# Attention and two gated layers on one core: nine groups of instructions put behind later ones in the order of emission

## The chip, the cores and the metric

The kernel runs on one core of a Trainium2 chip. The metric is the device time of one execution in microseconds (us). A core has five engines that work at the same time, each through its own instructions in order: PE (matrix products), DVE (VectorE), ACT (ScalarE), POOL (GpSimd) and SP (here only the queue that issues transfers). They wait for each other, and for transfers, through semaphores.

## What is computed

```python
# attention: a window of 15 keys to each side, and the 24 block summaries of all keys
k_sum, v_sum = k blocks of 32: max, mean
a = softmax(concat([masked q k^T, q k_sum^T + log 32]))      # 2 batches, 8 heads, 768 rows, 64 wide
x = (a @ concat([v, v_sum]))                                 # 1536 tokens x 512
# first layer
xn = x / sqrt(mean(x * x) + 1e-6) * rms_g
x = (silu(xn @ w_gate) * (xn @ w_val)) @ w_out               # 512 -> 1536 -> 512
# second layer
h = x @ w_in2
out = where(h > 0, h, exp(min(h, 0)) - 1) @ w_out2           # 512 -> 2048 -> 512
```

The weights come as float64. Queries and keys are scaled so that the softmax is sharp.

## The kernel before

The 1536 tokens are three blocks of 512. Block 0 goes through both layers alone, chunk by chunk of 128 columns (`add_block1`, `add_block2`); blocks 1 and 2 go through them together afterwards, by seven products in place of eight (`add_joint`). Attention works on pairs of 64 query rows: the pair `j` of a batch is one score product (`scores`), and for each half `h` of the heads the row maxima (`row_max`, tile `nm`), the exponentials (`exps`, tile `e`, sums in `ss`), `guard` and `invert` (the factor `rs`), `normalize` (`e` times `rs`, on POOL or on DVE), four transposes (`turn_e`, tile `at`), a copy to SBUF (`copy_e`, tile `ats`), then the product with the values (`apply_v2`, tile `pv`) and a copy into the block (`copy_x2`, tile `xT`). The names carry batch, pair and half: `e_2_0` is the third pair's first half. Pairs 0 to 3 of batch 0 are block 0; pair 4 is the first of block 1.

A product in float32 is made of three: each operand is split in a high part (`x_hi` for the block, `split_a` for a weight) and what is left (`x_lo`, `split_b`), tiles `xs` and `ws`. Block 0 is split in halves of 256 tokens, since its first two chunks (`pg` for the gate, `pv_0c`, `pv_1c` for the value) start when the first half is there.

A weight of 128 x 512 float64 words is made float32 in four steps after its transfer (`st`): `convert_a` on ACT, `convert_b` on DVE (sign, exponent and all but three bits of the mantissa, into tile `raw`), `convert_c` for some, and `convert_d` on DVE, which adds the three lowest bits of the mantissa. `raw` is then split, and `keep` on SP writes it to HBM, from where blocks 1 and 2 load it again (`kept`).

The norm's root is found per half of block 0: two `square` on ACT, `sum_square` on PE (eight products with four columns each, tile `pss`), `mean_square` on DVE (`ms`), `root` on POOL (`y`), `diagonal` on DVE (`dg`), `spread` on PE (`prs`), `keep_root` (`rk`). For block 0 the root is not applied to `x`; it enters behind the first products, in `gate_r`, which needs both halves of `rk`.

The order of work is made by a planner (class `Order`): each group of instructions has an engine, a cost, a due time (shifted by the table `SHIFT`) and the tiles that it reads and writes. The planner plays the engines through time and appends each group to `started` when it begins; PSUM banks and buffers are given out in the same play. At the end of `Order.issue` the groups are emitted in the order of `started`:

```python
        for i in started:
            ops[i][3](*((taken[i],) if isinstance(ops[i][0], dict) else ()), *ops[i][4])
```

The engine's own order is the order of emission. The semaphores are set at emission too: an instruction waits for the last writer of what it reads, and for readers and writers of what it overwrites, as far as those have been emitted before it. A tile that takes over a PSUM bank or a buffer waits for the last user emitted before it.

Of the kernel before, what the change touches and what calls it, by code (L numbers as in the profile page):

```python
# [43 lines left out]
class Order:  # L44
# [18 lines left out]
    def add(self, engine, cost, due, fn, *args, r=(), w=(), new=()):  # L63

        due += SHIFT.get((fn.__name__, sum(due >= x for x in EDGES)), 0)
        self.ops.append((engine, cost, due, fn, args, tuple(r), tuple(w), tuple(new)))
# [15 lines left out]
    def issue(self):  # L82
        ops = self.ops
        n = len(ops)
        before = [set() for _ in range(n)]
        writer, readers, home, maker, users = {}, {}, {}, {}, {}
        queue = {}
        for i, (engine, _, due, _, _, r, w, new) in enumerate(ops):
            for tag, name in new:
                home[name] = tag  # L90
                if tag in self.slots and self.slots[tag][1]:
                    queue.setdefault(tag, []).append((due, i, name))
            for key in r:
                before[i].add(writer[key])
                readers.setdefault(key, []).append(i)
            for key in w:
                if key in writer:
                    before[i].add(writer[key])
                before[i].update(readers.pop(key, ()))
                writer[key] = i  # L100
            before[i].discard(i)
            for name in {key.split("#")[0] for key in (*r, *w)} | {name for _, name in new}:
                if name in home:
                    before[i].add(maker.setdefault(name, i))
                    users.setdefault(name, set()).add(i)
            before[i].discard(i)
        queue = {tag: [name for _, _, name in sorted(x)] for tag, x in queue.items()}
        after = [[] for _ in range(n)]
        left = [len(b) for b in before]
        for i, b in enumerate(before):  # L110
            for j in b:
                after[j].append(i)

        ready_at = [op[2] if op[0] in ("SP", "-") else 0.0 for op in ops]
        free = {tag: bufs for tag, (bufs, _) in self.slots.items()}
        busy, soon, started, port = dict(self.busy), {}, [], 0.0
        dma_free = now = 0.0
        events = [(t, -1, 0) for t in (*ready_at, *busy.values()) if t > 0]
        heapq.heapify(events)
        taken = [None] * n  # L120
        ticks = {}
        tiled = 0

        def offer(i):
            for engine in ops[i][0] if isinstance(ops[i][0], dict) else (ops[i][0],):
                soon.setdefault(engine, []).append(i)

        for i in range(n):
            if not left[i]:
                offer(i)  # L130


        def pick(i):
            need, found = {}, []
            for tags, name in ops[i][7]:
                for tag in tags if isinstance(tags, tuple) else (tags,):
                    n = need.get(tag, 0) + 1
                    if free[tag] >= n and (not self.slots[tag][1] or name in queue[tag][:n]):
                        break
                else:  # L140
                    return None
                need[tag] = n
                found.append((tag, name))
            return found

        def can(i):
            return pick(i) is not None

        def shared(i, engine):
            return engine in ("DVE", "POOL") and ops[i][3].__name__ in SHARED  # L150

        while len(started) < n or events:
            for engine in list(soon):
                if busy.get(engine, 0.0) > now + 1e-9:
                    continue
                todo = sorted((i for i in soon[engine] if taken[i] is None), key=lambda i: (ops[i][2], i))
                best = next((
                    i for i in todo if ready_at[i] <= now + 1e-9 and can(i)
                    and (not shared(i, engine) or port <= now + 1e-9)), None)
                if best is None:  # L160
                    continue
                where, cost, due, _, _, _, _, new = ops[best]
                if isinstance(where, dict):
                    cost = where[engine]
                look = now + self.look * cost
                if engine != "SP" and any(
                        ops[i][2] < due - self.urgent and now < ready_at[i] <= look and can(i) for i in todo):
                    continue
                taken[best] = engine
                for e in where if isinstance(where, dict) else (where,):  # L170
                    soon[e].remove(best)
                for tag, name in pick(best):
                    home[name] = self.tag_of[name] = tag
                    free[tag] -= 1
                    if self.slots[tag][1]:
                        queue[tag].remove(name)
                if engine == "SP":
                    dma_free = max(now + self.DMA_START, dma_free) + cost
                    busy[engine] = now + self.ISSUE.get(ops[best][3].__name__, 0.42)
                    end = dma_free + self.DONE.get(ops[best][3].__name__, self.DMA_DONE)  # L180
                else:
                    if engine == "PE":
                        name = ops[best][3].__name__
                        start = now
                        if TILED.get(name, 0) != tiled:
                            tiled = TILED.get(name, 0)
                            start += DRAIN_IN if tiled else DRAIN_OUT
                        end = self.pe_end(start, cost, LIGHT.get(name, 1.0), ticks)
                    else:
                        end = now + cost  # L190
                    busy[engine] = end
                if shared(best, engine):
                    port = end
                heapq.heappush(events, (end + (0.2 if engine == "PE" else 0.13), best, 1))
                heapq.heappush(events, (busy[engine], -1, 0))
                started.append(best)
                for j in after[best]:
                    left[j] -= 1
                    ready_at[j] = max(ready_at[j], end + self.hop(engine, ops[j][0]))
                    if not left[j]:  # L200
                        offer(j)
                        heapq.heappush(events, (ready_at[j], -1, 0))
            if not events:
                stuck = [(e, [(ops[i][2], ops[i][3].__name__, ops[i][4][:3]) for i in t[:3]]) for e, t in soon.items()]
                raise RuntimeError(f"no group can start: {stuck} {free}")
            now, i, ends = heapq.heappop(events)
            if ends:
                for name in {key.split("#")[0] for key in (*ops[i][5], *ops[i][6])} | {x for _, x in ops[i][7]}:
                    if name in users:
                        users[name].discard(i)  # L210
                        if not users[name]:
                            del users[name]
                            free[home[name]] += 1
        for i in started:
            ops[i][3](*((taken[i],) if isinstance(ops[i][0], dict) else ()), *ops[i][4])
        return now


# [1 line left out]
def fused_kernel(ctx: ExitStack, tc: tile.TileContext, q, k, v, w_gate, w_val, w_out, rms_g, w_in2, w_out2, out):  # L220
# [720 lines left out]
    def add_act(src, dst, due, tag="act"):  # L941
        h, l = dst + "h", dst + "l"
        add(ANY_SB, 0, due, act_a, src, dst, tag, r=[src], w=[h], new=[(tag, h)])
        add(ANY_2[ACT_B if "act1_0" in dst else 0], 0, due + 0.6, act_b, src, dst, tag, r=[src, h], w=[l], new=[(tag, l)])

# [641 lines left out]
X_0 = 23.0, 30.0  # L1587
WARM_AT = (3.4, 3.9, 4.0, 7.5, 8.5, 9.5, 10.5, 13.0)
AFTER_K, WARM_LONG = {1: 0, 2: 2}, {1: 8}
ACT_B = 0  # L1590
LO_0, LO_1 = (1, 1, 0), 0
LEN_A, LEN_2, LEN_U, LEN_P = 9.3, 6.3, 9.7, 1.37
# [40 lines left out]
```

## Time and profile before

| | |
|---|---|
| median of 3 runs | 590.31 us (589.70 to 591.51) |
| the profiled execution | 590.2 us, of which the instructions span 588.4 |
| PE busy | 575.3 us (98%) |
| DVE busy | 543.4 us (92%) |
| ACT busy | 408.4 us (69%) |
| POOL busy | 97.1 us (17%) |
| granted TensorE clock | 1.0 in every slice |
| moved by transfers | 108.80 MB, 185 GB/s |

Times within the execution count from the start of the span. The profile calls a matrix product busy by a model of its end, so a busy PE may hold short waits. Its timeline lists instructions by start and length; lengths on one engine overlap a little, so the step from one start to the next is what an instruction costs its engine. "idle before" is the time in which the engine did nothing ahead of it, with the instruction whose end released it. The chain of waits follows the end of the program back through what released each step.

### The profile page before, as it was taken

The page shows a single profiled execution, that of the slowest core. Times are in us where ns is not written, and L with a number is a line of the kernel's source. Part 1 is how long each engine was busy: PE and PEld are TensorE (multiplying, and loading weights), DVE is VectorE, ACT ScalarE, POOL GpSimd, SP SyncE. Part 2 cuts the span into 40 slices and gives each one's busy share as a digit, 9 for nine tenths or more (in the row PEclk, how much of TensorE's full clock was granted, in tenths as well). Part 3 has the DMA queues.
Part 4 walks back from the last instruction along what each step waited for, and adds up shares of the span by engine and source line. Part 5 has one row for each costly group of instructions (what it writes and reads, how often), then busy time and mean ns, then how long its engine had stood idle before and what let it go on. Part 6 is the DMA issues. An engine that isn't in the chain of part 4 may idle for free.

```text
span 588.4 us, 10067 instructions
## 1 busy us (share of the span) xinstructions
PE 575.3 (98%) x3382; PEld 469.9 (80%) x3382; DVE 543.4 (92%) x1048; ACT 408.4 (69%) x888; POOL 97.1 (17%) x144
## 2 busy tenths in 40 slices
PE   7899999999999999999999999999999999999997
PEld 3688877888888888888888888788888888888886
DVE  4999988889999997999989888999999999999994
ACT  4887749755989888375455446596667599977651
POOL 5655466453311104000000000000000000000000
PEclk9999999999999999999999999999999999999999
DMA  9688997769778699223533453331206625816021
GB/s 318 227 282 299 321 381 279 252 204 298 251 260 299 230 378 342 99 101 116 178 107 108 144 164 123 90 108 55 72 19 206 187 73 173 261 58 207 1 72 53
DMA packets 56052, 108.80 MB, mean 185 GB/s; under 512 B 6784, under 2 KB 19584, under 8 KB 56000
## 3 DMA queue, kind: packets, MB, share of 16 engines
q1 hardware_dynamic: 56000, 108.16, 55.4%
q8 instruction: 26, 0.43, 0.3%
q14 instruction: 26, 0.21, 0.1%
HBM read 79.82 MB, written 28.31 MB: 184 GB/s over the span
## 4 chain that ended last, share of the span: by engine, by line
PE 87%; DVE 7%; ACT 3%; issue 1%; DMA 1%; POOL 0%; DVEq 0%; ACTq 0%; POOLq 0%
PE acc L952 13%; PE ph L896 8%; PE B_1u L1123 7%; PE B_2u L1123 6%; PE B_2d L1302 6%; PE A_1u L1123 5%; PE C_1u L1123 5%; PE B_1d L1302 4%; PE pg L896 4%; PE A_2u L1123 4%; PE C_2d L1302 4%; PE C_2u L1123 4%; PE A_2d L1302 4%; PE C_1d L1302 3%; ACT e L670 2%; PE A_1d L1302 2%
## 5 line engine op out<-in xcount | busy, mean ns | idle before, releaser
L1123 PE MATMUL B_1u<-xh,w_1u 128*128 128x512 f32 x144 | 48.9, 389 | 0.0
L896 PE MATMUL ph<-xa,ws_i 128*128 128x512 f32 x192 | 45.9, 392 | 0.0
L896 PEld LDWEIGHTS ph<-xa,ws_i 128*128 128x128 f32 x192 | 35.7, 188 | 7.7 <-issue 0.2
L896 PE MATMUL pg<-xs,ws_g 128*128 128x512 f32 (+1 forms) x168 | 36.9, 366 | 0.2 <-DVE th L920 0.2
L1123 PE MATMUL C_1u<-xh,w_1u 128*128 128x512 f32 x96 | 33.4, 390 | 1.1 <-DVE c_1u L1115 1.1
L303 ACT CAST wd<-rd 128x512 fp32r<-128x512 f32 x49 | 29.6, 618 | 5.5 <-PE A_1d L1302 2.8
L1123 PE MATMUL A_1u<-xh,w_1u 128*128 128x512 f32 x96 | 33.2, 389 | 0.0
L314 DVE TENSOR_TENSOR wd<-rd,wd 128x512 fp32r<-128x512 f32 x49 | 33.0, 684 | 0.0
L1302 PE MATMUL B_2d<-td,wd 128*128 128x512 f32 x144 | 32.8, 389 | 0.0
L1123 PE MATMUL B_2u<-xh,w_2u 128*128 128x512 f32 x96 | 32.8, 391 | 0.0
L896 PEld LDWEIGHTS pg<-xs,ws_g 128*128 128x128 f32 x168 | 27.9, 189 | 5.8 <-POOL ws_g L314 0.6
L1302 PEld LDWEIGHTS B_2d<-td,wd 128*128 128x128 f32 x144 | 27.0, 188 | 5.6
L1123 PEld LDWEIGHTS B_1u<-xh,w_1u 128*128 128x128 f32 x144 | 27.0, 188 | 5.6
L303 ACT CAST td<-z 128x512 fp32r<-128x512 f32 x28 | 16.7, 620 | 16.9 <-DVE z L1284 16.7
L1123 PE MATMUL B_1u<-xl,w_1u 128*128 128x512 f32 x72 | 28.0, 389 | 0.0
L685 POOL TENSOR_TENSOR e<-e,rs 128x480 f32<-128x480 f32 x20 | 21.3, 1070 | 38.8 <-ACT ex L930 16.7
L670 ACT ACTIVATE e<-e,nm 128x120 f32<-128x120 f32 x64 | 24.4, 385 | 0.9 <-DVE nm L663 0.9
L1302 PE MATMUL B_1d<-td,wd 128*128 128x512 f32 x108 | 24.6, 389 | 0.0
L1302 PEld LDWEIGHTS B_1d<-td,wd 128*128 128x128 f32 x108 | 20.3, 188 | 4.2
L303 ACT COPY h_1u<-B_1u 128x512 f32<-128x512 f32 x22 | 12.9, 588 | 14.8 <-PE B_1u L1123 13.5
L1302 PE MATMUL A_2d<-td,wd 128*128 128x512 f32 x96 | 22.2, 389 | 0.0
L1123 PEld LDWEIGHTS C_1u<-xh,w_1u 128*128 128x128 f32 x96 | 18.0, 188 | 5.3 <-DVE c_1u L1115 1.6
(530 smaller groups left out, 1770.2 us busy)
## 6 DMA issues: line engine op xcount, KB each, us to landing
st_i<-in_moe_w_in SPq DMA_DIRECT2D x16, 512.0 KB, 4.9
st_p<-in_moe_w_out SPq DMA_DIRECT2D x16, 512.0 KB, 5.4
st_v<-in_moe_w_val SPq DMA_DIRECT2D x12, 512.0 KB, 5.0
st_g<-in_moe_w_gate SPq DMA_DIRECT2D x12, 512.0 KB, 6.5
st_o<-in_moe_w_out SPq DMA_DIRECT2D x12, 512.0 KB, 5.2
kept_p<-raw_p SPq DMA_DIRECT2D x16, 256.0 KB, 5.1
kept_i<-raw_i SPq DMA_DIRECT2D x16, 256.0 KB, 5.2
va<-in_v SPq DMA_DIRECT2D x20, 192.0 KB, 6.4
```

Source lines behind the costliest of these rows:

```text
L303: nc.scalar.copy(out=out, in_=in_)
L314: (nc.gpsimd if eng == POOL else nc.vector).tensor_sub(out, a, b)
L670: nc.scalar.activation(out=e[:, pr, :], in_=s[:, pr, :], func=AF.Exp, bias=nm[:, pr:pr + 1], accum_out=ss[:, pr:pr + 1])
L685: nc.gpsimd.tensor_mul(e, e, rs.unsqueeze(2).to_broadcast([P, NP, NK]))
L896: nc.tensor.matmul(pt[:, i], wt[:, a, kk * P:(kk + 1) * P], xt[:, c, i], start=(kk == 0 and n == 0), stop=(kk == KM - 1 and n == 2))
L952: nc.tensor.matmul(acc, wt[:, a, cs], ot[e], start=(first and n == 0), stop=(last and n == 2))
L1123: nc.tensor.matmul(pt, wt[:, a, cs], xt[e][:, kk], start=first and kk == n == 0, stop=kk == 1 and n == 2, skip_group_check=not first)
L1302: nc.tensor.matmul(pt[:, h], wt[:, a, cs], xt[:, e, h], start=first and n == 0, stop=last and n == 2 and h.stop == TB, skip_group_check=i ...
```

## The change

A table `HOLD` names nine groups, each with another that starts later in `started`. A named group is left out at its own place and emitted right behind its partner; the planner's play, and with it which bank or buffer each tile gets, stays as it was.

```diff
+        def find(name, *some):
+            return next(i for i in started if ops[i][3].__name__ == name and set(some) <= set(map(str, ops[i][4])))
+
+        held = {}
+        for late, first in HOLD:
+            held.setdefault(find(*first), []).append(find(*late))
+        later = {j for x in held.values() for j in x}
+
+        def emit(i):
+            ops[i][3](*((taken[i],) if isinstance(ops[i][0], dict) else ()), *ops[i][4])
+            for j in held.get(i, ()):
+                emit(j)
+
         for i in started:
-            ops[i][3](*((taken[i],) if isinstance(ops[i][0], dict) else ()), *ops[i][4])
+            if i not in later:
+                emit(i)
...
+HOLD = [
+    (("normalize", "0", "2_0"), ("row_max", "0", "3_0")),
+    (("sum_square", "0", "slice(0, 256, None)"), ("project", "pv0_0c", "slice(256, 512, None)")),
+    (("mean_square", "0", "slice(0, 256, None)"), ("copy_e", "0", "4_0")),
+    (("root", "0", "slice(0, 256, None)"), ("mean_square", "0", "slice(0, 256, None)")),
+    (("diagonal", "0", "slice(0, 256, None)"), ("convert_b", "g", "2")),
+    (("spread", "0", "slice(0, 256, None)"), ("project", "pg0_0", "slice(0, 256, None)")),
+    (("convert_d", "v", "0"), ("x_lo", "xT0", "3", "slice(0, 256, None)")),
+    (("convert_d", "g", "0"), ("x_lo", "xT0", "3", "slice(0, 256, None)")),
+    (("keep_root", "0", "slice(0, 256, None)"), ("convert_d", "o", "2")),
+]
```

Line numbers behind the first hunk grow by 14. On DVE, the third pair's normalization (`e_2_0`), before:

```order
L314 TENSOR_TENSOR ws_v_469<-raw_v_406,ws_v_469 128x512
L687 TENSOR_TENSOR e_2_0_415<-e_2_0_415,rs_2_0_536 128x480
L676 TENSOR_SCALAR ss_2_1_508<-ss_2_1_508 128x4
L680 RECIPROCAL rs_2_1_580<-ss_2_1_508 128x4
L663 TENSOR_REDUCE nm_3_1_585<-s_3_1_532 128x4
L663 TENSOR_REDUCE nm_3_0_587<-s_3_0_519 128x4
L305 COPY xT_269<-pv_0_563 128x4x128
```

and now:

```order
L328 TENSOR_TENSOR ws_v_469<-raw_v_406,ws_v_469 128x512
L690 TENSOR_SCALAR ss_2_1_508<-ss_2_1_508 128x4
L694 RECIPROCAL rs_2_1_579<-ss_2_1_508 128x4
L677 TENSOR_REDUCE nm_3_1_584<-s_3_1_532 128x4
L677 TENSOR_REDUCE nm_3_0_586<-s_3_0_519 128x4
L701 TENSOR_TENSOR e_2_0_415<-e_2_0_415,rs_2_0_536 128x480
L319 COPY xT_269<-pv_0_562 128x4x128
```

The normalization went behind the fourth pair's two maxima. On DVE, the low parts of block 0's first half (`xs`) and the conversions (`raw_v_683` is value chunk 0, `raw_g_699` gate chunk 0, `raw_g_687` gate chunk 1), before:

```order
L442 TENSOR_SCALAR raw_g_699<-st_g_378 128x512
L455 SCALAR_TENSOR_TENSOR raw_v_683<-st_v_517,raw_v_683 128x512
L455 SCALAR_TENSOR_TENSOR raw_g_699<-st_g_378,raw_g_699 128x512
L876 SCALAR_TENSOR_TENSOR xs_0_681<-xT_269,g_sb,xs_0_681 128x256
L790 TENSOR_SCALAR ms0slice(0, 256, None)_745<-pss0slice(0, 256, None)_702 128x2
L876 SCALAR_TENSOR_TENSOR xs_1_685<-xT_269,g_sb,xs_1_685 128x256
L876 SCALAR_TENSOR_TENSOR xs_2_694<-xT_269,g_sb,xs_2_694 128x256
L876 SCALAR_TENSOR_TENSOR xs_3_696<-xT_269,g_sb,xs_3_696 128x256
L455 SCALAR_TENSOR_TENSOR raw_g_687<-st_g_217,raw_g_687 128x512
L806 TENSOR_SCALAR dg0slice(0, 256, None)_794<-ident,y0slice(0, 256, None)_749 128x128 x2
L659 SCALAR_TENSOR_TENSOR e_4_0_727<-s_4_0_725,mask_156 128x480
```

and now:

```order
L456 TENSOR_SCALAR raw_g_699<-st_g_378 128x512
L890 SCALAR_TENSOR_TENSOR xs_0_681<-xT_269,g_sb,xs_0_681 128x256
L890 SCALAR_TENSOR_TENSOR xs_1_685<-xT_269,g_sb,xs_1_685 128x256
L890 SCALAR_TENSOR_TENSOR xs_2_694<-xT_269,g_sb,xs_2_694 128x256
L890 SCALAR_TENSOR_TENSOR xs_3_696<-xT_269,g_sb,xs_3_696 128x256
L469 SCALAR_TENSOR_TENSOR raw_v_683<-st_v_517,raw_v_683 128x512
L469 SCALAR_TENSOR_TENSOR raw_g_699<-st_g_378,raw_g_699 128x512
L469 SCALAR_TENSOR_TENSOR raw_g_687<-st_g_217,raw_g_687 128x512
L673 SCALAR_TENSOR_TENSOR e_4_0_716<-s_4_0_714,mask_156 128x480
```

The four low parts now stand in a row, both conversions follow them, and the root's steps have left this place. The split of `raw_v_683` (`split_a` on ACT, `split_b` on POOL) and its `keep` on SP are emitted ahead of its `convert_d` now. They take the tile as `convert_b` left it, without the three lowest bits of the mantissa, in the products of block 0 and in the kept copy alike. `convert_d` of this tile waits for both readers: for `split_b` on POOL and for the end of the kept copy's transfer. `raw_g_699` is split later, as before.

On PE, around the first half's root in its new place, now (`pss`, `prs` first half, `ss0` and `rs0` second half):

```order
L910 MATMUL pv_0c<-xs_3_696,ws_v_707 128x256 x2
L799 MATMUL pss0slice(0, 256, None)_863<-ones,0, 1)slice(0, 256, None)_656 128x4 x2
L799 MATMUL pss0slice(0, 256, None)_863<-ones,2, 3)slice(0, 256, None)_677 128x4 x2
...
L910 MATMUL pg_0_943<-xs_3_696,ws_g_898 128x256 x3
L834 MATMUL prs0slice(0, 256, None)_956<-dg0slice(0, 256, None)_939,ones 128x256
L721 MATMUL pv_4_968<-ats_4_0_914,va_170 64x64
```

Before, the eight `pss` products stood between the transposes of `e_3_0` and the scores of pair 4, and `prs` between `pv_1c` and `pv_0c` of the first half. The banks make three waits that were not there: the second half's `sum_square` waits for the first half's `mean_square`, `spread` waits for the transposes of `e_4_0`, and `apply_v2` of pair 4 waits for the first half's `keep_root`.

## Rows read from the trace of the kernel before

**Rows 1.** Busy time by stretch: us, PE, weight loads, DVE, ACT, POOL, clock, DMA.
```profile
56.00:76.00 20.00, 20.00 (x99) 16.78 (x99) 19.93 (x41) 14.14 (x37) 7.97 (x9) 1.00 0.97 332
```

**Rows 2.** Waits of PE from 55 us to the end: total, times, longest.
```profile
PE C_1u L1123 <- DVE c_1u L1115: 1.1, 1, 1.1
PE pv L707 <- ACT ats L303: 0.2, 1, 0.2
```

**Rows 3.** Timeline of DVE, 14 to 46 us: start, length, instruction, idle before.
```profile
24.41 1.06 DVE L687 TENSOR_TENSOR e<-e,rs 128x480 f32<-128x480 f32 x1
...
26.07 1.19 DVE L663 TENSOR_REDUCE nm<-s 128x4 f32<-128x480 f32 x2
...
29.66 0.70 DVE L676 TENSOR_SCALAR ss<-ss 128x4 f32<-128x4 f32 x1 [0.46 <-ACT e L670]
...
30.56 0.66 DVE L305 COPY xT<-pv 128x512 f32<-128x512 f32 x1
```

**Rows 4.** Timeline of ACT, 14 to 46 us.
```profile
26.79 0.36 ACT L670 ACTIVATE e<-s,nm 128x120 f32<-128x120 f32 x1 [2.29 <-DVE nm L663]
...
31.25 0.64 ACT L773 ACTIVATE )slice(0, 256, None)_656<-xT 128x512 f32<-128x512 f32 x1 [0.60 <-DVE xT L305]
...
33.98 0.57 ACT L303 COPY ats<-at 120x512 f32<-120x512 f32 x1
...
37.82 0.62 ACT L303 CAST ws_g<-raw_g 128x512 fp32r<-128x512 f32 x1 [0.42 <-DVE raw_g L455]
```

**Rows 5.** Timeline of PE, 14 to 46 us.
```profile
28.51 1.15 PE L707 MATMUL pv<-ats,va 120*64 120x64 f32 x30 [0.21 <-DVE ats L305]
...
32.85 0.51 PE L785 MATMUL 0slice(0, 256, None)_702<-ones,)slice(0, 256, None)_656 128*128 128x4 f32 x4
...
34.62 1.05 PE L654 MATMUL s<-ka,q 64*64 64x120 f32 x32
35.60 1.15 PE L707 MATMUL pv<-ats,va 120*64 120x64 f32 x32
...
42.17 1.60 PE L896 MATMUL pv_0c<-xs,ws_v 128*128 128x256 f32 x12
43.61 1.60 PE L896 MATMUL pg<-xs,ws_g 128*128 128x256 f32 x12
```

**Rows 6.** Timeline of PE, 45 to 80 us.
```profile
45.05 1.34 PE L695 MATMUL at<-ident,e 128*120 128x128 f32 x8
46.23 0.51 PE L785 MATMUL lice(256, 512, None)_928<-ones,lice(256, 512, None)_834 128*128 128x4 f32 x4
...
47.93 1.68 PE L896 MATMUL pg<-xs,ws_g 128*128 128x256 f32 x12
49.54 1.15 PE L707 MATMUL pv<-ats,va 120*64 120x64 f32 x32
50.62 0.70 PE L820 MATMUL lice(256, 512, None)_995<-lice(256, 512, None)_990,ones 128*128 128x256 f32 x2
50.97 1.77 PE L896 MATMUL pg<-xs,ws_g 128*128 128x256 f32 x12
```

**Rows 7.** Timeline of DVE, 14 to 46 us: low parts, conversion, root copy.
```profile
37.03 0.75 DVE L455 SCALAR_TENSOR_TENSOR raw_g<-st_g,raw_g 128x512 uint16<-128x512 uint16 x1
...
39.76 0.41 DVE L305 COPY rk<-0slice(0, 256, None)_808 128x256 f32<-128x256 f32 x1
...
40.65 1.66 DVE L876 SCALAR_TENSOR_TENSOR xs<-xT,g_sb,xs 128x256 fp32r<-128x256 f32 x4
```

**Rows 8.** Timeline of POOL, 14 to 46 us: `split_b` of value chunk 0.
```profile
35.15 1.28 POOL L314 TENSOR_TENSOR ws_v<-raw_v,ws_v 128x512 fp32r<-128x512 f32 x1 [3.37 <-ACT ws_v L303]
```

**Rows 9.** Timeline of SP, 28 to 45 us: issues ahead of the kept copy.
```profile
32.00 0.78 SPq L606 DMA_DIRECT2D va<-in_v  x2
```

**Rows 10.** Landing times of `kept_v`: the one issued from 33 to 36 us.
```profile
DMA to landing us min/median/max: 3.9/3.9/3.9
```

**Rows 11.** Landing times of `kept_v`: the three issued from 30 to 60 us.
```profile
DMA to landing us min/median/max: 3.9/7.8/8.4
```

## Prediction

> **What bounds the kernel now.** I read the busy times first, then the stretches, then the timelines of the four engines where the moves are. From 56 to 76 us PE is busy 20.00 of 20.00 us and DVE 19.93 [rows 1]: whatever arrives late at 50 us stays late, because PE has no idle time to make it up with. After 55 us the profile has four waits of PE, 1.1 us for DVE and three of 0.2 us [rows 2], 1.7 together. That is all the slack there is, so the change is judged by when PE reaches the second product of gate chunk 0, which starts at 50.97 [rows 6].
>
> Ahead of that, two things set the pace. Up to 35 us PE waits for attention's chain: ACT idles 2.29 us until the fourth pair's first maximum at 26.79, and 0.60 until DVE has copied the second pair's output at 31.25 [rows 4]. That copy is at 30.56, behind a `guard` that waited 0.46 for ACT [rows 3]. From 35 us on PE does the first products one after the other, 1.44 us for twelve (42.17, 43.61, 45.05) [rows 5, 6].
>
> **Part 1: the third pair's normalization.** It takes DVE from 24.41, 1.06 long [rows 3]. Without it the fourth pair's maxima start about 0.88 before 26.07 (one length less its overlap and a `guard` that POOL may hold up), and ACT, which idles there, starts its exponentials as much earlier. The `guard` at 29.66 then has nothing to wait for. The copy behind it is bounded by `pv_1`, whose product ends at 28.51 + 1.15 = 29.66 [rows 5]: late `e_2_0` makes its transposes join those of `e_2_1`, which stand directly ahead of `pv_1`, so I add 0.09 and put the copy at 29.75, 0.81 earlier. ACT's squares follow it, from 31.25 to 30.43, and ACT works without a pause from there to the copy `ats_3_0`, 33.98 + 0.57 = 34.55 [rows 4], now 33.73. The scores of pair 4 take the bank that this copy frees; they start at 34.62 [rows 5], now at 33.80. **Gain 0.82 us.**
>
> **Part 2: `sum_square` of the first half.** It ran on PE from 32.85 to 34.62, 1.77 us [rows 5], just while the scores had to wait for ACT until 34.55. Taking it out gains nothing. In the new place nothing covers it: 1.75 us of PE are added between two dense products.
>
> **Part 3: the conversions.** Low parts first is cheap: four take 1.66 us where POOL is quiet [rows 7]. But value chunk 0 is now split and written away ahead of its `convert_d`, so DVE has to wait with it for `split_b` and for the landing of the kept copy, a wait that is new. `split_b` starts at 35.15 and takes 1.28 [rows 8]; 0.82 earlier it ends at 35.61. The copy needs SP, which is done with two issues at 32.00 + 0.78 [rows 9], somewhat earlier with pair 3, so I put its issue at 32.45. The copy now in that place lands after 3.9 us [rows 10]; so 36.35. I take it for its like surroundings. The other two of the kind take 7.8 and 8.4 [rows 11], which is the far end.
>
> The Trainium skill (DMA: Bandwidth & Descriptors, Anatomy of one DMA) gives about 2.0 us and bytes over 436 GB/s for a transfer: 2.6 us for 256 KB, as an estimate. The row says 3.9, so here the page is short by half; by the page the copy would land at 35.05, POOL would end the wait at 35.65, and the sum would be the second rival's.
>
> Behind the wait on DVE stand the other conversions and pair 4's masks and maxima. Gate chunk 1's conversion is third in the row: at steps of 0.65 and a length of 0.75 [rows 7] it ends at 36.4 + 2.05 = 38.45, where it ended at 37.78 before. Its cast on ACT takes 0.62 [rows 4] and `split_b` 1.28 as above: the low weights are there at 40.45. PE comes to that product at 33.80 + 0.98 + 1.09 + 1.44 + 1.44 = 38.75 (scores, `pv_3`, two products; steps of [rows 5]). It can do two of twelve steps of 0.12, then it waits until 40.5: **1.5 us of PE idle**. SP's fetches of the next chunks, which wait for these conversions, go out about 1.6 us later; I cost them at nothing, as ACT converts them only behind pair 4's exponentials. If that cover were gone it would show as ACT waiting for `st`.
>
> From 40.5: ten steps 1.2, the value product 1.44, `sum_square` 1.75, the gate product 1.5 (the first behind tiny products is slower: 1.61 from 47.93 to 49.54 [rows 6]). The transposes of pair 4 start at 46.4 in place of 45.05: 1.35 late, with part 1's gain already in it.
>
> **Part 4: the root's second stage.** The second half's `sum_square` has the same bank, so it waits for the first half's `mean_square`, behind the copy of `ats_4_0` on DVE. From transposes to `sum_square` it was 46.23 - 45.05 = 1.18; four transposes (0.67, half of 1.34 [rows 6]), the copy (0.66 like the one in [rows 3]) and `mean_square` (0.1, an estimate for two columns) end 1.45 behind, so 0.27 more. `sum_square` takes 1.70 (46.23 to 47.93 [rows 6]): the first gate product of chunk 0 starts at 46.4 + 1.45 + 1.70 = 49.55, 1.62 late.
>
> From that start to the second product it was 50.97 - 47.93 = 3.04 [rows 6]. Now `spread` of the first half is put between: product 1.6, `spread` until its result 0.70 [rows 6], `keep_root` on DVE 0.41 [rows 7], and only then `pv_4`, which takes over the bank, 1.08. That makes 3.88 with two hops. Meanwhile DVE, which stood behind `keep_root`, has a conversion (0.65), `convert_b` and the second `diagonal` (0.8 for both, an estimate from one conversion with its length of 0.75 [rows 7]) to do before the second `spread` can start, at 4.15, and the product follows 0.35 later: 4.5. So 1.46 more, of which 0.35 is work and the rest waiting. What DVE and POOL do for this root stays the same; `root` on POOL is covered, as POOL is 17% busy in all.
>
> **The sum.** 1.62 + 1.46 = 3.08, which I round to 3.0: part 1 is in it with its 0.82. PE and DVE are dense after that [rows 1], so it reaches the end. The profiled execution took 590.2, 0.1 below the median of 590.31; **590.2 + 3.0 = 593.2 us**. What a measurement of this kernel can tell from no change is about 0.3%, 1.8 us.
>
> **Rivals.**
>
> *The late slack takes it (same, 591.5).* If DVE recovers its lateness where it has idle time after 76 us, the waits of PE for it shrink by up to 1.7 us [rows 2]: 593.2 - 1.7 = 591.5, not slower by 0.3%. Its place is the 1.1 us wait for `c_1u` and the three short ones; it decides if DVE arrives there less late than PE does. Against it: these waits are for DVE work that depends on PE's own late products. Chance 0.19.
>
> *The copy lands before POOL is done (slower, 592.5).* Then the wait ends at 35.65, 0.7 earlier, and so does all that hangs on it: 593.2 - 0.7. The Trainium skill's transfer time, above, would make it so; the trace's 3.9 [rows 10] speaks against it. Chance 0.15.
>
> *The copy lands like the other two (slower, 597).* 7.8 us [rows 11] instead of 3.9 is 3.9 more on the same path. For it: it goes out among value and weight loads. Against it: those two were issued after 39 us, with more in front of them. Chance 0.05.
>
> *The root's second stage is hidden (faster, 589.4).* Part 1 alone gives 590.2 - 0.8. It would need PE not to wait for chunk 1's weights and the root's bank waits to fall in pauses; the first needs the conversion of value chunk 0 to start by 34.7, and POOL alone ends at 35.61. Chance 0.07.
>
> *Forecast* as above: 0.54, with a range of its own from 592.2 to 594.8.
>
> **How the numbers follow.** Faster is the fourth rival, 0.07. The same is the first rival and a little of the forecast's lower edge, 0.21. Slower is the rest, 0.72. The range goes from 590.8 (late slack and early landing together: 593.2 - 1.7 - 0.7) to 594.8 (a landing 1.6 later than I take); outside are the late landing, 0.05, the faster case, 0.07, and the edges.
>
> **What would show it.** Right: the exponentials of pair 3 start near 25.9 and the scores of pair 4 near 33.8; DVE idles from about 34.6 to 36.4 ahead of a conversion, released by the kept copy; PE idles about 1.5 us inside the first gate product of chunk 1, near 39 to 40.5; `sum_square` of the first half near 43; `pv_4` waits about half a microsecond for `keep_root`; the second gate product of chunk 0 starts near 54. Wrong: DVE does not stop at the conversion, or PE reaches that product before 52, or is late there and not late at 80 us.

## Result, and the profile after

The changed kernel takes 598.76 us (median of 4 runs, 598.49 to 600.32), the kernel before 590.74 beside it on the same chip: ratio 1.0139, 95% interval 1.0121 to 1.0156. It is slower, as forecast, but by some 8 us where 3 were forecast, and lies outside the range. The profiled execution took 599.01, 8.8 more than that of before (590.2).

When the same work starts on PE in both traces says where the time went:

| start of | before, us | after, us | late by | forecast |
|---|---|---|---|---|
| scores of pair 3 | 23.31 | 22.85 | -0.46 | 0 |
| scores of pair 4 | 34.62 | 33.52 | -1.10 | -0.82 |
| transposes of pair 4 | 45.05 | 49.11 | 4.06 | 1.35 |
| first product of gate chunk 0 | 47.93 | 52.64 | 4.71 | 1.62 |
| second product of gate chunk 0 | 50.97 | 58.59 | 7.62 | 3.08 |
| scores of pair 6 | 83.50 | 92.26 | 8.76 | 3.0 |
| the long run of products in the last stage (`A_2d`) | 511.23 | 520.09 | 8.86 | 3.0 |

Everything is lost between 34 and 92 us, and from there to the last stage only 0.1 more.

Single executions already differ ahead of the first change: the scores of pair 3, in front of which all these kernels do the same, start at 22.85 in this one, at 23.31 in that of before, and between 22.85 and 24.98 in the profiled executions of this document. Where it matters I count from there.

The timeline of PE after, 22 to 62 us (start, length, instruction, idle before and its releaser), answers to [rows 5, 6]:

```profile
26.98 1.06 PE L709 MATMUL at<-ident,e 128*120 128x128 f32 x8 [2.00 <-ACT e L684]
...
33.52 1.52 PE L668 MATMUL s<-ka,q 64*64 64x120 f32 x32 [0.46 <-ACT xT L317]
...
40.30 0.50 PE L910 MATMUL pg<-xs,ws_g 128*128 128x256 f32 x2 [1.11 <-ACT ws_g L317]
41.66 2.26 PE L910 MATMUL pg<-xs,ws_g 128*128 128x256 f32 x10 [0.86 <-POOL ws_g L328]
43.73 2.33 PE L910 MATMUL pv_0c<-xs,ws_v 128*128 128x256 f32 x12
45.89 0.50 PE L799 MATMUL 0slice(0, 256, None)_863<-ones,)slice(0, 256, None)_656 128*128 128x4 f32 x4
...
49.11 1.03 PE L709 MATMUL at<-ident,e 128*120 128x128 f32 x8
50.65 0.58 PE L799 MATMUL lice(256, 512, None)_922<-ones,lice(256, 512, None)_815 128*128 128x4 f32 x4 [0.50 <-DVE 0slice(0, 256, None)_916 L804]
...
52.64 2.91 PE L910 MATMUL pg<-xs,ws_g 128*128 128x256 f32 x12
55.34 0.74 PE L834 MATMUL 0slice(0, 256, None)_956<-0slice(0, 256, None)_939,ones 128*128 128x256 f32 x2
56.60 1.15 PE L721 MATMUL pv<-ats,va 120*64 120x64 f32 x32 [0.52 <-DVE rk L319]
58.27 0.67 PE L834 MATMUL lice(256, 512, None)_995<-lice(256, 512, None)_990,ones 128*128 128x256 f32 x2 [0.51 <-DVE lice(256, 512, None)_990 L820]
58.59 1.77 PE L910 MATMUL pg<-xs,ws_g 128*128 128x256 f32 x12
```

All the forecast waits are there, at their places: at the first product of gate chunk 1 (1.11 and 0.86, together 1.97 where 1.5 were forecast), and three half microseconds around the root. What was not forecast stands in the lengths. A product of twelve steps took 1.6 before [rows 5, 6]; here it is 2.33 at 43.73 and 2.91 at 52.64. The stretches tell why (busy us of PE, weight loads, DVE, ACT, POOL; granted clock; DMA share; GB/s):

```profile
24.00:27.00 3.00, 1.00 (x33) 0.89 (x31) 2.90 (x7) 1.51 (x9) 2.92 (x5) 1.00 0.43 130
27.00:30.00 3.00, 2.91 (x41) 2.55 (x41) 2.09 (x8) 2.17 (x10) 1.50 (x4) 0.72 0.00 1
30.00:33.00 3.00, 3.00 (x40) 2.41 (x40) 2.50 (x7) 2.67 (x7) 0.87 (x1) 0.71 0.81 269
40.00:42.00 2.00, 0.84 (x4) 0.64 (x5) 1.93 (x5) 2.00 (x6) 1.28 (x1) 0.99 1.06 395
42.00:44.00 2.00, 2.00 (x12) 2.00 (x11) 1.64 (x6) 2.00 (x10) 0.00 (x0) 0.50 0.69 213
44.00:46.00 2.00, 2.00 (x14) 2.00 (x13) 1.76 (x5) 2.00 (x10) 1.35 (x1) 0.65 1.08 414
52.00:54.00 2.00, 2.00 (x12) 2.00 (x12) 1.56 (x4) 0.00 (x0) 0.88 (x1) 0.55 0.00 0
54.00:56.00 2.00, 2.00 (x10) 1.68 (x8) 0.00 (x0) 0.00 (x0) 0.14 (x1) 0.59 0.59 180
```

Behind PE's pause of 2.00 us, behind the two in gate chunk 1, and behind the half-microsecond pause and the short products of `sum_square`, TensorE runs part of the time at the lower of its two levels, 1.2 in place of 2.4 GHz. Before, the granted clock is 1.00 in these stretches.

The timeline of DVE after, 24 to 58 us, answers to [rows 3, 7]:

```profile
24.77 1.19 DVE L677 TENSOR_REDUCE nm<-s 128x4 f32<-128x480 f32 x2
25.88 0.96 DVE L701 TENSOR_TENSOR e<-e,rs 128x480 f32<-128x480 f32 x1
...
37.61 0.76 DVE L469 SCALAR_TENSOR_TENSOR raw_v<-st_v,raw_v 128x512 uint16<-128x512 uint16 x1 [2.94 <-DMA kept_v<-raw_v]
...
56.12 0.42 DVE L319 COPY rk<-0slice(0, 256, None)_956 128x256 f32<-128x256 f32 x1 [2.50 <-PE 0slice(0, 256, None)_956 L834]
```

The timeline of SP after, 30 to 50 us, has the issue of the kept copy, behind those of [rows 9]:

```profile
32.05 0.78 SPq L620 DMA_DIRECT2D va<-in_v  x2
32.93 0.38 SPq L483 DMA_DIRECT2D kept_v<-raw_v  x1
```

The chain of waits after has its way to the landing:

```profile
32.93 4.58 DMA kept_v<-raw_v
```

It landed 4.58 us later, at 37.51; DVE stood still for it from 34.67 to 37.61.

### The profile page after: what moved, and what is told of

Same layout as the page of the kernel before. It is cut to its first block, busy times and chain, and to the rows that moved or that the text cites. A ratio compares the mean times of both kernels' runs of the same rounds, so it can differ in the third digit from the quotient of the medians.

```text
span 597.3 us, 10071 instructions
## 1 busy us (share of the span) xinstructions
PE 580.1 (97%) x3382; PEld 473.9 (79%) x3382; DVE 545.2 (91%) x1048; ACT 408.3 (68%) x888; POOL 96.9 (16%) x144
## 4 chain that ended last, share of the span: by engine, by line
PE 83%; DVE 7%; DMA 4%; ACT 3%; issue 1%; SPq 0%; POOL 0%; DVEq 0%; ACTq 0%
PE acc L966 13%; PE ph L910 7%; PE B_1u L1137 7%; PE B_2u L1137 6%; PE B_2d L1316 5%; PE A_1u L1137 5%; PE C_1u L1137 5%; PE B_1d L1316 4%; PE C_2d L1316 4%; PE C_2u L1137 4%; PE A_2u L1137 4%; PE A_2d L1316 4%; PE pg L910 4%; PE C_1d L1316 3%; ACT e L684 2%; PE A_1d L1316 2%
## 5 line engine op out<-in xcount | busy, mean ns | idle before, releaser
L910 PE MATMUL pg<-xs,ws_g 128*128 128x512 f32 (+1 forms) x168 | 39.4, 384 | 2.8 <-ACT ws_g L317 1.1
L910 PEld LDWEIGHTS pg<-xs,ws_g 128*128 128x128 f32 x168 | 29.9, 205 | 9.0 <-POOL ws_g L328 1.6
```

Of the source, the lines that this page charges most:

```text
L910: nc.tensor.matmul(pt[:, i], wt[:, a, kk * P:(kk + 1) * P], xt[:, c, i], start=(kk == 0 and n == 0), stop=(kk == KM - 1 and n == 2))
```

## The experiments

The numbers of "rows" in the expectations count the nine entries of `HOLD`: 1 is the normalization, 2 to 6 and 9 the root, 7 and 8 the conversions of value chunk 0 and gate chunk 0. The edits are against the changed kernel. A ratio is to the kernel before on the same chip: 591.3 us (median of 14 runs) for e1_norm to e4_no_v0, 590.67 (8 runs) for e5_readers, e6_keep_late, e7_clock and e9_spread, 590.94 (15 runs) for the other four.

### The parts alone

**e1_norm**

```diff
 HOLD = [
     (("normalize", "0", "2_0"), ("row_max", "0", "3_0")),
-    (("sum_square", "0", "slice(0, 256, None)"), ("project", "pv0_0c", "slice(256, 512, None)")),
...
-    (("keep_root", "0", "slice(0, 256, None)"), ("convert_d", "o", "2")),
```

> Only the third pair's normalization is moved; the eight other groups stand as before. By the forecast's part 1 the fourth pair's scores start 0.8 us earlier and nothing else changes: about 589.9 us against 590.7. The rival, read from the trace of the changed kernel: PE waits 2.0 us at 25 to 27 us for the late third pair, the granted clock of 27 to 33 us falls to 0.7 as it did there, and what the maxima gain is given back: 590.5 to 592.

Measured: 590.64 us, 0.999 (0.9972 to 1.0008): no difference that can be told, where 0.8 was forecast. In the profiled execution PE waits 1.92 us at 28.28, and the clock is 0.89 and 0.54 in the two stretches behind it; the scores of pair 4 come 11.63 us after those of pair 3 (11.31 before). Over the ten runs, five with a mean clock of 1.00 average 590.29 us, five at 0.996 to 0.997 average 591.39.

**e2_root**

```diff
 HOLD = [
-    (("normalize", "0", "2_0"), ("row_max", "0", "3_0")),
...
-    (("convert_d", "v", "0"), ("x_lo", "xT0", "3", "slice(0, 256, None)")),
-    (("convert_d", "g", "0"), ("x_lo", "xT0", "3", "slice(0, 256, None)")),
```

> Only the six entries of the root of block 0's first half are moved. By the forecast's steps (1.75 us of sum_square in the open, the bank waits of sum_square, of the fourth scores' output and of the second spread) it is 2 to 3 us slower, 593 to 594, at a full clock. If the lowered clock belongs to this part, the stretch of the first gate product of chunk 0 (50 to 56 us) shows a granted clock near 0.6 and it is 594 to 595.

Measured: 594.37 us, 1.0054 (1.0035 to 1.0073), 3.1 to 3.2 us more. The clock is 1.00 in every stretch, the second product of gate chunk 0 starts at 53.90, and the three waits of half a microsecond are there. So the root's move costs 3 us by itself; the profiled execution had no help from the clock in it.

**e3_conv** and **e4_no_v0**

The first keeps the two conversions alone, the second all but that of value chunk 0:

```diff
 HOLD = [
-    (("normalize", "0", "2_0"), ("row_max", "0", "3_0")),
...
     (("convert_d", "v", "0"), ("x_lo", "xT0", "3", "slice(0, 256, None)")),
     (("convert_d", "g", "0"), ("x_lo", "xT0", "3", "slice(0, 256, None)")),
-    (("keep_root", "0", "slice(0, 256, None)"), ("convert_d", "o", "2")),
```

```diff
-    (("convert_d", "v", "0"), ("x_lo", "xT0", "3", "slice(0, 256, None)")),
```

> Only the two conversions are moved; the values of value chunk 0 lack their three lowest mantissa bits, as in the changed kernel. DVE stops until the kept copy has landed, near 37.5 us; chunk 1's gate conversion ends 1.8 us later than before. Theory of the wait: 1.8 us slower, 592.5. Theory of wait and clock: PE idles over 1 us ahead of that gate product, the granted clock of the 3 to 4 us behind it is near 0.5, and 1.5 us more are lost: 594. If the lost time of the changed kernel belongs to the root alone, no change: 590.7.

> All entries but the conversion of value chunk 0, which goes back ahead of its readers (all mantissa bits are there again, and nothing waits for the kept copy). Theory of the wait: DVE does not stop, PE does not idle at 39 to 41.7 us and the clock does not fall behind it; left are part 1's gain and the root's cost, 592 to 593.5. If the root's waits alone lower the clock, 50 to 56 us still shows about 0.6: 593.5 to 594.5. If the copy's wait matters little, it stays at 597 to 599.

Measured: e3_conv 595.03 us, 1.0062 (1.0046 to 1.0078), a microsecond above the theory of wait and clock; e4_no_v0 595.03, 1.0060 (1.0037 to 1.0083), scattered from 593.40 to 596.52, above the theories in which the wait matters (594.5 at most) and below the one in which it does not. With the root in its old place the late conversions hold up the spread of the first half on PE for 2.4 us, and the clock falls to 0.50 from 42 to 44. Without the conversion of value chunk 0 DVE does not stop; of the 8 us that the change costs, 3.7 go by the medians and 4.7 by the ratios. In its profiled execution, one of the two fastest, PE still waits 0.70 in gate chunk 1, and the clock is 0.63 and 0.52 from 50 to 54. The parts, e1_norm, e2_root and e3_conv, are 0, 3.1 and 3.7: together some 7, which the intervals don't tell from 8.

### The wait for the kept copy

**e6_keep_late**

```diff
+    (("keep", "v", "0"), ("convert_d", "v", "0")),
 ]
```

> The change with all nine entries, and the write of the kept copy of value chunk 0 put behind the late conversion; the two splits stay ahead of it, so the three lowest mantissa bits of value chunk 0 are missing in its split, as in the change. DVE then waits for POOL's low part alone, which ended at 35.82 in the changed kernel, where the copy landed at 37.5. Theory (the landing sets the length of the wait): the conversion at about 35.9, 1.7 earlier, PE's pause in the first gate product of chunk 1 shorter by as much (0.3 to 0.5 left of 1.97), and 596 to 597; a little less if the clock then holds. Rival (POOL is late anyway, and the landing only just later): 598 to 599.

Measured: 595.77 us (594.13 to 597.92), 1.0091 (1.0065 to 1.0117), 3 us better than the change by the medians. In the profiled execution, the fastest of the four, DVE now waits for POOL alone, by its timeline:

```profile
35.74 0.77 DVE L469 SCALAR_TENSOR_TENSOR raw_v<-st_v,raw_v 128x512 uint16<-128x512 uint16 x1 [1.17 <-POOL ws_v L328]
```

It starts 1.87 earlier than after the change, PE's pauses in gate chunk 1 shrink to 0.86, and the clock is 1.00 from 38 to 50 us. So the landing sets the wait, and more hangs on it than its own length: the fall of the clock behind PE's pause goes too.

**e5_readers**

```diff
+    (("split_a", "ws0_v0"), ("convert_d", "v", "0")),
+    (("split_b", "ws0_v0"), ("split_a", "ws0_v0")),
+    (("keep", "v", "0"), ("convert_d", "v", "0")),
 ]
```

> The change with all nine entries, and three more that put the readers of value chunk 0 (its cast on ACT, its low part on POOL, its way out to DRAM) behind the late conversion. So DVE waits neither for the kept copy nor for POOL, and the chunk is split whole, as before. Theory (3.7 us of the change are this one wait on DVE, with the lowered clock that its pause on PE brings): the conversion runs at 34.7, the low weights of value chunk 0 are ready at about 37.4, just ahead of the product at 37.6, those of gate chunk 1 at about 38.7, PE has no pause there, the granted clock stays at 1.00 from 36 to 50 us; the second gate product of chunk 0 starts near 54 and the time is 594 to 595. Rival (the value chunk's later split is itself late for its product, or holds up ACT): PE waits at 37.6 for it and the time is 596 or more. Rival (the wait only uncovers others): no better than 598.

Measured: 596.52 us (595.90 to 600.50), 1.0116 (1.0082 to 1.0150). The theory's 594 to 595 was a miss, and the first rival right. The profiled execution is the slowest of the four, with pair 3's scores at 24.98, so it shows where the waits are and not what the others took. DVE doesn't stop, but the cast of value chunk 0 now stands on ACT behind another conversion, which waits for its fetch (timeline of ACT, 34 to 44 us):

```profile
38.84 0.69 ACT L448 ACTIVATE st_o<-st_o 128x512 f32<-128x512 f32 x1 [2.60 <-DMA st_o<-in_moe_w_out]
39.43 0.60 ACT L317 CAST ws_v<-raw_v 128x512 fp32r<-128x512 f32 x1
```

PE then waits 0.84 for that chunk's low weights and 1.22 for those of gate chunk 1. In both orders tried behind the low parts the conversion is late for somebody: as a writer it waits for its readers, ahead of them they wait for it.

### The clock

**e7_clock** and **e12_clock_all**

The first has idle products in `project`, the second those and others in `turn_e`:

```diff
 def project(name, tag, ws, x, kks, i):
...
+        if name == "pg0_1" and i.start == 0:
+            for _ in range(8):
+                nc.tensor.matmul(pt, idle_w, idle_w.unsqueeze(1).to_broadcast([P, 4, P]), start=True, stop=True)
...
 def turn_e(b, t, tag):
...
+        if b == 0 and t == "2_0":
+            for _ in range(8):
+                nc.tensor.matmul(pt, idle_w, idle_w.unsqueeze(1).to_broadcast([P, 4, P]), start=True, stop=True)
```

> The changed kernel with eight idle products of 128 x 512 on PE ahead of the first half of gate chunk 1's first product, in the bank that this product then overwrites; no result hangs on them. They fill most of the 1.97 us in which PE waits there. Theory (about 2.7 us of the miss are the lowered clock behind the pause): the granted clock stays at 1.00 from 40 to 50 us, ten steps and the next product take 2.6 in place of 4.2, and the time falls by 1.6 to 2.7, to 596 to 597. Rival (the clock falls for another reason, or the time is lost in waits whatever the clock): the time stays at 598 to 599, or rises by what the idle products take.

> The whole change, with both fillings: eight idle products ahead of the first transpose of pair 3, and eight ahead of gate chunk 1's first product. Theory (the clock costs the change 2 to 2.7 us in all, what is left are waits): granted clock 1.00 in every stretch from 20 to 62 us, mean clock 0.999 or more in every execution, 596 to 597 us, and less scatter than the one filling (596.6 to 600.24). So some 6 us over before stay as waits, twice the forecast's 3.0. Rival (the lowered clock near 30 us costs the change nothing, as DVE then waits for the copy anyway): the same 597.1 as with the one filling.

Measured: e7_clock 597.13 us (596.60 to 600.24), 1.0123 (1.0096 to 1.0150); e12_clock_all 597.29 (596.11 to 597.66), 1.0104 (1.0089 to 1.0119), whose interval lies wholly below the change's. The profiled execution of e7_clock took 596.60, 2.4 less than that of the change, and its granted clock is 1.00 where it had been 0.50 to 0.65; by the intervals of the times alone e7_clock can't be told from the change. Its timeline of PE, 39 to 57 us:

```profile
39.77 1.90 PE L909 MATMUL pg<-idle_w 128*128 128x512 bf16 x8
41.32 0.59 PE L913 MATMUL pg<-xs,ws_g 128*128 128x256 f32 x2
42.29 1.45 PE L913 MATMUL pg<-xs,ws_g 128*128 128x256 f32 x10 [0.39 <-POOL ws_g L328]
43.58 1.60 PE L913 MATMUL pv_0c<-xs,ws_v 128*128 128x256 f32 x12
...
48.25 1.03 PE L709 MATMUL at<-ident,e 128*120 128x128 f32 x8
...
51.56 1.68 PE L913 MATMUL pg<-xs,ws_g 128*128 128x256 f32 x12
53.08 0.59 PE L834 MATMUL 0slice(0, 256, None)_964<-0slice(0, 256, None)_947,ones 128*128 128x256 f32 x2
...
56.17 1.78 PE L913 MATMUL pg<-xs,ws_g 128*128 128x256 f32 x12
```

From 42.29 to `sum_square` at 45.02 are 2.73 us, 4.23 in the change; from 42.29 to the last product shown 13.88, 16.93 in the change. The second filling gains nothing that can be told over the first, as its rival said. In the profiled execution of e12_clock_all the clock is 1.00 up to 52 us and 0.50 from 54 to 56, where its theory had 1.00, so that fall is not tied to the pauses that were filled. The executions at a clock of 0.999 or more (596.60 and 596.87; 597.45, 596.11 and 597.66) are still 5.2 to 6.7 us slower than before. So of the 8.0 that the change loses by its median the clock is 1.3 to 2.8 by these times; the rest is lost at full clock too. The two traces say more: counted from pair 3's scores (22.85 and 24.32) to the end, the change takes 3.9 us longer than e7_clock.

### The root's second stage, and the first part again

**e9_spread** and **e11_spread_warm**

Entries 5, 6 and 9 stay, in the second run with three idle products ahead of the transposes in `turn_e`:

```diff
 HOLD = [
-    (("normalize", "0", "2_0"), ("row_max", "0", "3_0")),
-    (("sum_square", "0", "slice(0, 256, None)"), ("project", "pv0_0c", "slice(256, 512, None)")),
-    (("mean_square", "0", "slice(0, 256, None)"), ("copy_e", "0", "4_0")),
-    (("root", "0", "slice(0, 256, None)"), ("mean_square", "0", "slice(0, 256, None)")),
...
-    (("convert_d", "v", "0"), ("x_lo", "xT0", "3", "slice(0, 256, None)")),
-    (("convert_d", "g", "0"), ("x_lo", "xT0", "3", "slice(0, 256, None)")),
```

```diff
+        if b == 0 and t == "4_1":
+            for _ in range(3):
+                nc.tensor.matmul(pt, idle_w, idle_w.unsqueeze(1).to_broadcast([P, 4, P]), start=True, stop=True)
```

> Of the root only its second stage is moved: the diagonal, the spread and the copy of the result of the first half, rows 5, 6 and 9 of the table. The sums of the first half stay in their old place in the pause of PE. Theory (the steps of the prediction: 1.46 us for the second stage, of which 0.35 is work and the rest two waits in a chain over DVE; the first stage costs 2.0 for the sums in a dense stretch): the second gate product of chunk 0 starts at about 52.4, the granted clock stays at 1.00, and the time is 591.5 to 592. Rival (the late slack takes a shift of this size): 590 to 590.6. Rival (nearly all of the root's 3.1 us is the second stage): 593 or more.

> The second stage of the root alone (rows 5, 6 and 9, as in the run before it with 593.08), with three idle products of 128 x 512 on PE ahead of the transposes of e_4_1, in the bank that these overwrite; they fill the 0.71 us in which PE waits there. Theory (of that run's 2.4 us about 1.0 is the clock that is lowered from 48 to 52 us, and 1.5 the two waits and the work of the second stage): the granted clock stays at 1.00 from 46 to 54 us, the second gate product of chunk 0 starts about 29.6 us behind the scores of pair 3 (30.67 without the idle products, 27.66 before), and the time is 592.0 to 592.4. Rival (the waits cost the 2.4 at any clock): 593 or more.

Measured: e9_spread 593.08 us, 1.0036 (1.0022 to 1.0050), over its theory's 592, with the clock at 0.66 and 0.50 from 48 to 52 in the slowest of its five executions; e11_spread_warm 593.19, 1.0039 (1.0025 to 1.0053), with the clock at 1.00 throughout. So the idle products held the clock and gained nothing: the expectation's rival holds. The forecast's step was of the right size all the same, by the timeline of PE of e11_spread_warm:

```profile
47.44 1.67 PE L913 MATMUL pg<-xs,ws_g 128*128 128x256 f32 x12
...
50.06 1.15 PE L724 MATMUL pv<-ats,va 120*64 120x64 f32 x32 [0.52 <-DVE rk L319]
51.72 0.67 PE L837 MATMUL lice(256, 512, None)_998<-lice(256, 512, None)_993,ones 128*128 128x256 f32 x2 [0.50 <-DVE lice(256, 512, None)_993 L823]
52.03 1.78 PE L913 MATMUL pg<-xs,ws_g 128*128 128x256 f32 x12
```

From the first gate product of chunk 0 to this last one are 4.59 us; the forecast has 4.5, and before it was 3.04. Counted from the scores of pair 3 (22.91) it is 29.12, 27.66 before: 1.46 more. That this is the forecast's own figure for the second stage is luck, as what PE saves where `spread` stood and what it loses around the transposes of pair 4 happen to cancel. The rest comes later: PE waits 0.6 for `B_1u` from ACT, a wait that before does not have. A lateness at 50 us is not carried to the end as it is.

**e8_norm_warm** and **e10_no_norm**

The first is entry 1 alone with the eight idle products in `turn_e` that e12_clock_all has; the second leaves out entry 1:

```diff
-    (("normalize", "0", "2_0"), ("row_max", "0", "3_0")),
```

> Row 1 alone (the normalization behind the maxima), with eight idle products of 128 x 512 on PE ahead of the first transpose of pair 3, in the bank that this transpose then overwrites; they fill most of the 1.9 us in which PE waits there for the late normalization. Theory (row 1 gains about 0.8 us, and a lowered clock behind its pause takes it back in those executions in which the clock falls; row 1 alone gave 590.3 in the five executions at a mean clock of 1.00 and 591.4 in the five at 0.996 to 0.997): the granted clock is 1.00 from 27 to 33 us, the scores of pair 4 start about 10.5 us behind those of pair 3 (before 11.31, row 1 alone 11.63), and the time is about 0.5 to 0.8 below that of before, 589.8 to 590.2. Rival (the gain goes elsewhere, in waits that do not depend on the clock): within 0.2 of before.

> The change without row 1: root and conversions moved, the normalization where it was. Theory (row 1 gains 0.5 to 0.8 us of earlier scores, as forecast, whatever stands behind it): 599.2 to 599.6, so 0.5 to 0.8 above the change's 598.76. Rival (with DVE stopped until the kept copy lands, earlier scores of pair 4 only wait longer, and the pause of PE that row 1 makes near 25 us costs clock): the same as the change or down to 597.5, and DVE's idle time ahead of the conversion is shorter than 2.94.

Measured: e8_norm_warm 590.59 us, 1.0002 (0.9991 to 1.0013), with a mean clock of 0.999 or more in all eleven runs. The scores of pair 4 come 10.98 us after those of pair 3, 0.33 sooner than before, and yet nothing is gained. The next wait shows why, first in the timeline of PE of e8_norm_warm:

```profile
25.07 1.90 PE L710 MATMUL at<-idle_w 128*128 128x512 bf16 x8
26.97 1.09 PE L712 MATMUL at<-ident,e 128*120 128x128 f32 x8
...
38.47 0.70 PE L837 MATMUL 0slice(0, 256, None)_816<-0slice(0, 256, None)_802,ones 128*128 128x256 f32 x2 [0.73 <-DVE e L673]
```

and in that of before:

```profile
38.76 0.70 PE L820 MATMUL 0slice(0, 256, None)_808<-0slice(0, 256, None)_794,ones 128*128 128x256 f32 x2 [0.38 <-DVE e L659]
```

The first half's `spread` takes a bank of pair 4's scores, which DVE frees with its masks, and DVE stands behind its conversions. PE waited 0.38 there before, 0.73 now: the 0.33 are given back in this one wait. The theory that only the clock eats the gain falls. e10_no_norm gave 597.49 us, 1.0114 (1.0097 to 1.0131), 1.3 below the change by the medians: inside the change the normalization's move costs, as the rival said. DVE's stop is 2.49 us there. The two intervals overlap, so the size is not settled.

No version beats the kernel before; entry 1, with or without the idle products, equals it.

## Why the prediction was wrong in size, point by point

**Part 1, the gain of 0.82: the exponentials right, the gain wrong.** They started at 25.49, 1.30 sooner, 0.46 of it the execution's earlier pair 3. The step that failed is the gain's way to the end: e1_norm and e8_norm_warm show none. It took for granted that earlier scores of pair 4 move all behind them, while the first half's spread waited for DVE already.

**Part 2 and the root's second stage: the steps right, the end not.** In e2_root, at full clock, `sum_square` took 1.70 (42.75 to 44.45; forecast 1.75), the way from transposes to first product 3.32 (forecast 3.15) and from there to the second 4.61 (forecast 4.5). The scores of pair 4 came 0.5 sooner there without the sums ahead of them (10.82 us behind those of pair 3, 11.31 before): a small gain where the prediction saw none. That its 3.1 us come so near to the forecast's 1.75, 0.27 and 1.46 less this gain is luck: at the second product, counted from pair 3's scores, it is only 2.71 late, since `spread` has left its old place, and the rest is lost behind, where the forecast has nothing.

**Part 3, the landing at 36.35: the wait right, its size wrong.** The copy was issued at 32.93 (taken: 32.45) and took 4.58 (taken: 3.9, [rows 10]), so it landed 1.16 later, and the low weights of gate chunk 1 were there at 41.66 in place of 40.5. The issue stands behind that of `va`, which waits for PE and was taken to come earlier; it came at 32.05, 32.00 before. In four more kernels with this order, e3_conv, e7_clock, e10_no_norm and e12_clock_all, the landing took 4.5, 4.5, 4.2 and 5.7. The Trainium skill (DMA: Bandwidth & Descriptors, Anatomy of one DMA), by which I had estimated 2.6 us, a third less than the row, is further off than it; that section has its figures for transfers issued by GpSimd, and this one is issued on SP. The prediction's second rival, "the copy lands before POOL is done", is what e6_keep_late built: its conversion at 35.74 stands 0.1 from the rival's 35.65. Its time, 595.77, is still 3.3 above the rival's 592.5, so the landing is not all that the sum lacks. The term that the prediction put at nothing here, the later fetches, held: the next one of `st_o` went out at 38.39 (35.44 before), and ACT did not wait for it.

**The term that was missing: the clock.** This is the step that failed most: the prediction costed each pause of PE at its own length. In the change's trace a lowered clock follows them. From 41.66, when the low weights are there, to the second product of chunk 0 at 58.59 are 16.93 us; e7_clock, with the same order at a clock of 1.00, takes 13.88. So the clock costs 3.05 in this execution: 1.50 up to `sum_square` (4.23 against 2.73), and most of the rest in the product at 52.64 (2.70 to its successor, 1.52 in e7_clock). The forecast's own steps make 13.55, so at full clock they were 0.33 short, around the root. The fall from 27 to 33 us is in the landing as well: the copy is issued 10.08 us behind pair 3's scores in the change and 9.23 in e7_clock and e12_clock_all, whose clock is 1.00 there; the forecast has 9.14. In the times, filling the pauses gave back less, 1.5 to 2.4.

**"It reaches the end" as it stands: wrong.** Behind 58.59 another 1.2 us are lost. DVE stands idle for 2.50 us at 56.12, behind the slow product, and the chain of waits runs over DVE from there to 69.23, where it stops PE; before has no wait of PE there. The slow product isn't needed for it: in e2_root and e7_clock, at full clock, DVE stands idle for 1.08 and 1.09 at this place, PE has the same wait (0.62 and 0.65), and 1.1 and 1.3 are lost behind the second product. But e4_no_v0, e6_keep_late, e10_no_norm and e12_clock_all don't have the wait and lose at most 0.4, so what decides it stays open. Timeline of PE after:

```profile
69.27 1.66 PE L910 MATMUL pg<-xs,ws_g 128*128 128x512 f32 x6 [0.61 <-DVE th L934]
```

The first rival had the late slack giving up to 1.7 us back; it took 1.2 more. The waits of PE after 55 us, beside [rows 2], with total, times and longest:

```profile
PE C_1u L1137 <- DVE c_1u L1129: 1.1, 1, 1.1
PE pg L910 <- DVE th L934: 0.8, 2, 0.6
```

The wait for `c_1u` has kept its 1.1.

The sum, against the forecast's 3.08: 1.16 for the landing, 3.05 for the clock, 0.33 for the steps around the root, 1.2 behind: 5.7, with 3.08 8.8, which is what the profiled executions differ by. That the landing sets the wait is shown by e6_keep_late, the second term by the trace of e7_clock, though the times of e7_clock and e12_clock_all give it a smaller share, the third by e2_root and e7_clock, the last by traces alone.

What stays open: the clock's fall between 48 and 58 us, which e4_no_v0, e5_readers, e6_keep_late, e9_spread, e10_no_norm and e12_clock_all have and e2_root and e7_clock, with the same three waits, have not. No run isolates it.

## What to carry to other kernels

When work is moved behind the readers of its buffer, it inherits their waits, a transfer's landing among them; count that wait, and everything queued behind it on that engine. A pause that is put into a dense stretch of PE can cost more than its length, as the products behind it may run at the lower clock: give it a price range up to a doubling of the next few products (in e3_conv twelve steps behind a pause of 2.4 us took 2.89 where they take 1.44 at full clock). And a gain at one point is worth nothing until the next wait on the path is found: look which engine is awaited there already.

## What the runs showed of the hardware that was not expected

Pauses alike did not always lower the clock. PE's pause of 2 us near 25 us was followed by 0.72 and 0.71 in the change, by 0.89 and 0.54 in e1_norm and by 0.99 and 0.50 in e5_readers, but by 1.00 in e4_no_v0, e6_keep_late and e7_clock, with waits of 1.9 to 2.0 at the same transposes. In e9_spread it was 0.69 and 0.74 there with no pause of that length, only 0.45, 0.85 and 0.21; before, with 0.17, 1.10 and 0.21, the clock is 1.00. Eight idle products of 1.90 us in it (e8_norm_warm) kept the mean clock at 0.999 or more in eleven of eleven runs, where e1_norm without them had it in five of ten, and the kernel before beside it in eleven of fifteen.
